# One-pass fillers of 512 columns for TensorE, at other places, and a later fourth weight piece

## The chip, the cores and the metric

The kernel runs on one core of a Trainium2 chip. The metric is the device time of one execution in microseconds (us); the median of three runs stands for it, 677.03 us before the change. A profile of one execution, with every instruction's start and duration, goes with it.

## What is computed

Two blocks in a row. The first is a gated linear recurrence over 768 steps, for 4 batches and 8 heads of 48 channels, with a complex gate for each step and channel; the second is a layer with one hidden activation, x·cos(x).

```python
mag = sqrt(a_re * a_re + a_im * a_im)
scale = minimum(mag, 0.999) / (mag + 1e-06)
a = (a_re + 1j * a_im) * scale             # per batch, head, step, channel
for t in range(S):                         # S = 768
    state = a[t][:, None] * state + outer(k[t], v[t])
    y[t] = q[t] @ real(state)
x = y, heads side by side                  # 3072 x 384
h = x @ w_in                               # 384 -> 2048
out = (h * cos(h)) @ w_out                 # 2048 -> 384
```

The inputs are float32, but the two weights arrive as 64-bit floats and are turned into 32-bit ones on the chip.

## The kernel before, in words

The steps are cut into chunks of 128 and two chunks make a group: 24 chunks, 12 groups. Within a chunk the recurrence is turned into matmuls: cumulative sums of the log gate and of its angle (products with a triangular matrix: `lgs` and `phs` in PSUM), keys and queries scaled by powers, cosines and sines of them (`ks`, `qs`), their transposes (`kT`, `qT`), the scores (`sc`), a masked copy of those (`atm`), the state that is carried on (`sp`, `state`), and the outputs. In group 0 these come as rows (`yr`, copied to `rows`) and are transposed (`xp`) to columns (`xT`); in later groups they are made as columns (`yp`). The second block is `mm1` (`hp`, eight pieces jp of 256 hidden columns, then cosine on ScalarE, a square sum `junk` on ScalarE, and a product on VectorE into `gate`) and `mm2` (`op`).

Nearly everything up to the first full group is a long prologue, and the change lies in it. What sets its order:

- `matmul` (L683) chains every TensorE instruction to the one before it, so TensorE runs in the order in which the program lists it. ScalarE's special functions are chained too. As long as `Ordered.by_hand` is true (L1225 to L1247), so is all of VectorE and ScalarE. After that a scheduler orders VectorE's and ScalarE's other work by where it is listed and by which operands it needs; each engine then takes its instructions strictly in that order.
- The weights are fetched in 16 pieces of 768 KB by GpSimd's DMA queue, eight of `w_in` (0 to 7 here) and eight of `w_out` (8 to 15), into four buffers (`raw`). A piece is converted in four steps (`as_floats`, L619): a shift and an or on VectorE (`TENSOR_SCALAR`, `SCALAR_TENSOR_TENSOR`), an addition of a constant on ScalarE (`raw<-raw`), and a final addition on VectorE (`CUSTOM_DVE_ANT_0`). That frees the buffer for the piece four places later. Pieces 0 to 3 are `early[0]` to `early[3]`, listed by hand in the loop at L1248; the others are woven in from L1257 on.
- `busy(count)` (L686) issues TensorE products whose result nobody reads. They take a PSUM buffer of the five that `pa` has. Here they are full float32 products of two constants, 128 columns wide; a float32 product shows in the trace as two MATMUL records and two weight loads. The trace lists TensorE's granted clock, 1.00 or 0.50 of full speed.
- The calls of `busy`: 12 ahead of everything (L1227), 8 after the sums of each of the two chunks (L1233), 12 after the trigonometric steps (L1243).

Of the kernel before, what the change touches and what calls it, by code (L numbers as in the profile page):

```python
# [11 lines left out]
F32 = mybir.dt.float32  # L12
# [3 lines left out]
F32R = mybir.dt.float32r  # L16
# [471 lines left out]
def fast_path(ctx, tc, q, k, v, a_re, a_im, moe_w_in, moe_w_out, out, least, odd, wide):  # L488
# [6 lines left out]
    nc = tc.nc  # L495
    B, H, S, D = q.shape
    DM, DF = moe_w_in.shape
    C = 128
# [21 lines left out]
    stage = {"pool": room.enter_context(tc.tile_pool(name="stage", bufs=1)), "bufs": 4}  # L520
    pa = ctx.enter_context(tc.tile_pool(name="pa", bufs=5, space=PSUM))
# [11 lines left out]
    def constant(array, name, queue=nc.scalar, pool=consts):  # L533
        t = pool.tile(list(array.shape), F32, name=name)
        queue.dma_start(out=t, in_=nc.inline_tensor(array, name=name + "_const").ap())
        return t
# [13 lines left out]
    def load(g, names, i=None, put=nc.sync.dma_start):  # L550
        for name in names:
            ap = {"re": a_re, "im": a_im, "q": q, "k": k, "v": v}[name]
            if name not in X[g]:
                X[g][name] = ld.tile([C, G, H, D], F32, tag=name, name=name,
                                     bufs=2 if name == "v" else 1)
            b, c = divmod(g * G + (i or 0), NCH)
            one, n = i or 0, G if i is None else 1
            steps = ap[b].rearrange("h (c p) d -> p c h d", p=C)[:, ds(c, n)]
            tile_ = X[g][name][:, ds(one, n)]
            parts = [(0, C, 0)]  # L560
            if name in ("re", "im") and g >= PEG:

                parts = [(0, C - 16, 1), (C - 16, C - 1, 1)]
                put(out=tile_[C - 1:C], in_=steps[0:1])
            for i_ in range(n):
                for lo, hi, by in parts:
                    put(out=tile_[lo:hi, i_], in_=steps[lo + by:hi + by, i_])

    for names in ("re", "im"), ("k", "q"), "v":
        for i in range(G):  # L570
            load(0, names, i)
    ident = constant(np.eye(C, dtype=np.float32), "ident", pool=stage["pool"])
    sums = [constant(sums_np[0], "sums", pool=stage["pool"])]
# [20 lines left out]
    def weight(dst, src):  # L594
        if src.dtype == F32:
            nc.sync.dma_start(out=dst, in_=src)
            return lambda: None
        return from_double(dst, src)
# [50 lines left out]
    def chain(ins, engine="scalar"):  # L649

        if engine in tail:
            behind(ins, tail[engine])
        tail[engine] = ins
# [29 lines left out]
    def matmul(out, **kw):  # L683
        chain(nc.tensor.matmul(out, **kw), "tensor")  # L684

    def busy(count):  # L686

        ps = pa.tile([C, C], F32, tag="a", name="busy")
        for _ in range(count):
            matmul(ps, lhsT=ident, rhs=sums[0], start=True, stop=True)  # L690

    tables = {AF.Ln: "natural_log_exp_and_others", AF.Exp: "natural_log_exp_and_others",
              AF.Arctan: "trig_and_small", AF.Sin: "trig_and_small"}
# [2 lines left out]
    def preload(table):  # L696
        if loaded[0] != table:
            loaded[0] = table
            chain(nc.scalar.preload_act_table_set(table))  # L699
# [87 lines left out]
    def p_powers(g, i):  # L787

        x = X[g]
        if i == 0:  # L790
            x["P"], x["Q"] = x["lg"], temp("Q")
            x["row"] = rows_d.tile([G * DM], F32, tag="row", name="row")
            x["end"] = ft.tile([D2, G * H], F32, tag="end", name="end")
        ps = pa.tile([C, DM], F32, tag="a", name="lgs")
        summed_up(ps, g, i, "lg", sums[0])
        special(out=cut(x["P"], i, 1), in_=ps, func=AF.Exp)
        special(out=cut(x["Q"], i, 1), in_=ps, func=AF.Exp, scale=-1.0)
# [22 lines left out]
    def p_end(g, i, n):  # L820
        end = X[g]["end"][:, ds(i * H, n * H)]
        vector.tensor_scalar(out=end, in0=end, scalar1=-0.5, scalar2=None, op0=ALU.mult)
        low = least[:, ds(i * H, n * H)]
        vector.scalar_tensor_tensor(out=low, in0=end, scalar=LEAST, in1=low,
                                    op0=ALU.is_ge, op1=ALU.min)
# [40 lines left out]
    def g_trig(g, i, n):  # L866
        x = X[g]
        if i == 0:
            x["cos"] = temp("rs")
            if g:  # L870
                x["sin"] = temp("lg")
        cs, sn = cut(x["cos"], i, n), cut(x["sin"], i, n)
        ph = cut(x["tan"], i, n)
        vector.tensor_scalar(out=cs.bitcast(U32), in0=ph.bitcast(U32),
                                scalar1=0x7FFFFFFF, scalar2=None, op0=ALU.bitwise_and)
        special(out=sn, in_=ph, func=AF.Sin, scale=TWO_PI)
        special(out=cs, in_=cs, func=AF.Sin, scale=-TWO_PI, bias=half_pi_b)
# [44 lines left out]
    def queries(n, h):  # L922
        g, i = divmod(n, G)
        if g < PEG:
            return X[g]["qT"][:, i * H + h].rearrange("p q j -> p (q j)")
        return X[g]["qT"][:, :, i * H + h]
# [32 lines left out]
    def f_rows(n):  # L959

        y, (g, i) = Y[n], divmod(n, G)
        state = y.get("state")
        ps = pa.tile([C, H, D], F32, tag="a", name="yr")
        for h in range(H):
            matmul(ps[:, h], lhsT=y["atm"][:, h], rhs=X[g]["v"][:, i, h],
                   start=True, stop=(state is None))
            if state is not None:
                matmul(ps[:, h], lhsT=queries(n, h), rhs=state[:, h], start=False, stop=True)
        y["rows"] = msb.tile([C, DM], F32, tag="ot", name="rows")
        scalar.copy(out=y["rows"], in_=ps.rearrange("p h d -> p (h d)"))  # L970

    def f_columns(n):
        y, (g, i) = Y[n], divmod(n, G)
        ps = pa.tile([C, ND, C], F32, tag="a", name="xp")
        for c in range(ND):
            chain(nc.tensor.transpose(ps[:, c], y["rows"][:, ts(c, C)], ident), "tensor")
        if i == 0:
            X[g]["xT"] = msb.tile([C, ND, G, C], F32, tag="xT", name="xT")
        scalar.copy(out=X[g]["xT"][:, :, i], in_=ps)

    def f_state(n):
        if n % NCH == NCH - 1:
            return
        y, (g, i) = Y[n], divmod(n, G)
        ps = pa.tile([D2, H, D], F32, tag="a", name="sp")
        for h in range(H):
            keys = X[g]["ks"][:, i * H + h].rearrange("p a d -> p (a d)")
            matmul(ps[:, h], lhsT=keys, rhs=X[g]["v"][:, i, h], start=True, stop=True)
        new = ft.tile([D2, H, D], F32, tag="state", name="state")
        end = X[g]["end"][:, ts(i, H)].unsqueeze(2).to_broadcast([D2, H, D])  # L990
        if "state" in y:
            vector.scalar_tensor_tensor(out=new, in0=ps, scalar=0.25, in1=y["state"],
                                           op0=ALU.mult, op1=ALU.add)
            vector.tensor_tensor(out=new, in0=new, in1=end, op=ALU.mult)
        else:
            vector.scalar_tensor_tensor(out=new, in0=ps, scalar=0.25, in1=end,
                                           op0=ALU.mult, op1=ALU.mult)
        Y[n + 1]["state"] = new
# [162 lines left out]
    def turned(g, i, name):  # L1161
        return [lambda hh=hh: f_turn(g, i, name, hh) for hh in range(2)]
# [60 lines left out]
    early = [weight(dst, src) for dst, src in into[:RAW]]  # L1223
    chain(nc.gpsimd.tensor_copy(out=exact, in_=ones), "gpsimd")
    Ordered.by_hand = True  # L1225
    preload("natural_log_exp_and_others")
    busy(12)  # L1227
    one, two = (log_steps(0, i, 1) for i in range(2))
    for _ in range(5):
        next(one), next(two)  # L1230
    for i in range(2):
        p_powers(0, i)
        busy(8)  # L1233
    next(one), next(two)
    g_angle(0, 0, 2)
    for i in range(2):
# [3 lines left out]
    g_trig(0, 0, 1)  # L1240
    p_apply(0, 0, 1)
    g_trig(0, 1, 1)
    busy(12)  # L1243
    g_stack(0, 0, 1)
    p_apply(0, 1, 1)
    g_stack(0, 1, 1)
    Ordered.by_hand, Ordered.mark = False, dict(tail)  # L1247
    for t in (turned(0, 0, "kT") + turned(0, 0, "qT") + early[:1]  # L1248
              + [lambda: f_scores(0, 0), lambda: f_scores(0, 1)] + early[1:2]
              + turned(0, 1, "kT") + turned(0, 1, "qT") + early[2:3]  # L1250
              + [lambda: p_end(0, 0, 2), lambda: f_state(0), lambda: f_rows(0)] + early[3:4]
              + [lambda: f_scores(1, 0), lambda: f_scores(1, 1), lambda: f_columns(0)]
              + [lambda: f_state(1), lambda: f_rows(1), lambda: f_columns(1)]
              + [lambda: next(one, None), lambda: next(two, None),
                             lambda: load(2, ("v",))]):
        t()
# [95 lines left out]
```

## Time and profile before

| | |
|---|---|
| median of 3 runs | 677.03 us (676.07, 677.03, 678.66) |
| profiled execution, first to last instruction | 677.3 us |
| TensorE busy | 647.8 us, 96% |
| VectorE busy | 490.3 us, 72% |
| ScalarE busy | 396.4 us, 59% |
| granted clock below full speed | 11.8 to 15.2, 42.5 to 52.7, 69.8 to 73.2 us, and at the very end |

The profiled execution has no time of its own beside its span; the span lies 0.3 us above the median. "Idle before" in a line of the trace is written in brackets, with what ended it: `[0.94 <-DVE atm L673]` means that the engine sat idle for 0.94 us until VectorE had written `atm`. DVE is VectorE, ACT ScalarE, PE TensorE, PEld its weight load, POOL GpSimd, SP SyncE. All VectorE operations that go through the ordering helper carry its line, L673, and all matmuls L684, so they are told apart by their tiles.

### The profile page before, as it was taken

Reading aid. Unit: us, or ns where it says so; the run is one execution under the profiler, and the core shown is the slowest. Engines: PE = TensorE matmul, PEld = TensorE weight load, DVE = VectorE, ACT = ScalarE, POOL = GpSimd, SP = SyncE. Lnnn points to the kernel's source line nnn. Section 1 sums busy time; section 2 is a strip of 40 time slices with the busy share of each in tenths; the row PEclk is TensorE's granted clock in tenths of the full one; section 3 lists DMA queues with packets and bytes.
Section 4 is the critical chain, followed back from the end, with each engine's and each line's share of the span. In section 5 each row is a group of like instructions: output and inputs, shape, how many; then the busy total and the mean of one; then the engine's idle time right before and its main releaser. Section 6 shows DMA issues by size and latency. Waiting matters only on the chain.

```text
span 677.3 us, 10771 instructions
## 1 busy us (share of the span) xinstructions
PE 647.8 (96%) x4080; PEld 580.3 (86%) x4080; DVE 490.3 (72%) x792; ACT 396.4 (59%) x730; POOL 28.5 (4%) x47
## 2 busy tenths in 40 slices
PE   5788889999999999999999999999999999999995
PEld 5686657886799999999999999989999989999895
DVE  4879888759868778868768778868768769762251
ACT  5869775475466467367467467467367467432330
POOL 2011100000000000000000000000000000000000
PEclk8979899999999999999999999999999999999998
DMA  9778623923743864764864864854864753363000
GB/s 244 176 234 224 173 72 81 227 66 69 213 92 63 219 137 116 210 142 109 224 140 118 210 140 113 214 113 126 223 145 118 211 138 78 116 139 116 24 6 24
DMA packets 232810, 94.90 MB, mean 140 GB/s; under 512 B 208798, under 2 KB 221217, under 8 KB 232748
## 3 DMA queue, kind: packets, MB, share of 16 engines
q1 hardware_dynamic: 226252, 68.62, 44.5%
q0 software_dynamic: 5632, 25.17, 11.4%
q8 instruction: 34, 0.56, 0.4%
q10 hardware_dynamic: 864, 0.33, 0.2%
q14 instruction: 28, 0.23, 0.1%
HBM read 69.28 MB, written 24.81 MB: 139 GB/s over the span
## 4 chain that ended last, share of the span: by engine, by line
PE 79%; DVE 6%; DMA 6%; ACT 5%; issue 2%; SPq 1%; DVEq 0%; ACTq 0%
PE hp L684 32%; PE sum L684 15%; PE op L684 14%; PE yp L684 5%; PE sc L684 5%; PE sp L684 3%; PE phs L684 2%; DVE w_in L673 1%; PE lgs L684 1%; DMA raw<-in_moe_w_out_dram 1%; DMA xT<-x 1%; DMA qT<-moved 1%; DVE mag L673 1%; PE yr L684 1%; ACT L699 1%
## 5 line engine op out<-in xcount | busy, mean ns | idle before, releaser
L684 PE MATMUL hp<-xT,w_in 128*128 128x256 f32 x1152 | 254.2, 382 | 1.3 <-ACT xT L673 0.6
L684 PEld LDWEIGHTS hp<-xT,w_in 128*128 128x128 f32 x1152 | 219.9, 192 | 34.6 <-DMA xT<-x 1.9
L703 ACT ACTIVATE gate<-hp,half_pi_b 128x512 f32<-128x512 f32 x96 | 65.9, 686 | 128.0 <-PE hp L684 128.0
L673 DVE TENSOR_TENSOR gate<-hp,gate 128x512 f32<-128x512 f32 x96 | 65.5, 683 | 58.4 <-ACT junk L673 58.4
L684 PE MATMUL op<-w_out,gate 128*128 128x192 f32 (+1 forms) x448 | 103.0, 375 | 2.7 <-DVE w_out L673 2.7
L684 PEld LDWEIGHTS op<-w_out,gate 128*128 128x128 f32 x448 | 75.7, 190 | 19.7 <-DVE w_out L673 3.9
L673 ACT ACTIVATE junk<-hp 128x512 bf16<-128x512 f32 x96 | 56.5, 588 | 0.0
L684 PE MATMUL sum<-t_s,s 128*128 128x192 f32 x320 | 55.3, 326 | 0.0
L684 PEld LDWEIGHTS sum<-t_s,s 128*128 128x128 f32 x320 | 52.6, 190 | 0.0
L673 DVE TENSOR_TENSOR atm<-sc,causal 128x512 f32<-128x512 f32 x48 | 33.0, 687 | 25.4 <-PE sc L684 25.2
L684 PEld LDWEIGHTS sc<-qT,kT 96*128 96x128 f32 x384 | 47.6, 192 | 4.2 <-issue 2.2
L684 PE MATMUL sc<-qT,kT 96*128 96x128 f32 x384 | 49.4, 276 | 1.9 <-ACT qT L673 0.9
L673 ACT ACTIVATE ot<-sum 128x192 f32<-128x192 f32 x30 | 9.5, 320 | 49.4 <-PE sum L684 49.4
L699 ACT ACT_TABLE_LOAD x26 | 33.4, 1283 | 4.0 <-DMA ident<-ident_const 3.6
L673 ACT CAST tan<-phs 128x384 int32<-128x384 f32 x24 | 11.5, 479 | 39.7 <-PE phs L684 39.7
L673 DVE SCALAR_TENSOR_TENSOR ot<-op,ot 128x192 f32<-128x192 f32 x31 | 11.0, 354 | 32.3 <-ACT ot L673 23.5
L684 PE MATMUL yp<-atm,v 128*48 128x128 f32 x352 | 33.5, 277 | 0.0
L684 PEld LDWEIGHTS sp<-v,ks 128*96 128x96 f32 x320 | 29.7, 165 | 0.0
L684 PE MATMUL sp<-v,ks 128*96 128x48 f32 x320 | 29.6, 245 | 0.0
L684 PE MATMUL sum<-w_out,gate 128*128 128x192 f32 x160 | 29.6, 329 | 0.0
L684 PE MATMUL yp<-qT,state 96*48 96x128 f32 x304 | 29.6, 272 | 0.0
L684 PE MATMUL op<-t_a,gate 128*128 128x192 f32 x160 | 29.0, 332 | 0.0
(137 smaller groups left out, 992.7 us busy)
## 6 DMA issues: line engine op xcount, KB each, us to landing
moved<-tr SPq DMA_DIRECT2D x20, 768.0 KB
raw<-in_moe_w_in_dram POOLq DMA_DIRECT2D x16, 768.0 KB, 5.5
raw<-in_moe_w_out_dram POOLq DMA_DIRECT2D x16, 768.0 KB, 4.9
kT<-moved SPq DMA_DIRECT2D x40, 192.0 KB
qT<-moved SPq DMA_DIRECT2D x10, 768.0 KB
k<-in_k_dram SPq DMA_DIRECT2D x24, 192.0 KB
q<-in_q_dram SPq DMA_DIRECT2D x24, 192.0 KB
v<-in_v_dram SPq DMA_DIRECT2D x24, 192.0 KB
```

Of the source, the lines that this page charges most:

```text
L673: ins = getattr(self.engine, op)(**kw)
L684: chain(nc.tensor.matmul(out, **kw), "tensor")
L699: chain(nc.scalar.preload_act_table_set(table))
L703: chain(nc.scalar.activation(func=func, **kw))
```

## The change

The fillers become products in the one-pass format (`float32r`) of a tile of ones, 512 columns wide, instead of float32 products of the constants `ident` and `sums`. The tile `idle` is new and is set by VectorE ahead of its other first writes. The counts and places change: 27 at the start instead of 12; none between the two chunks' sums, and 10 after both instead of 8 and 8; 10 instead of 12 after the trigonometric steps; and three new groups around the second chunk's rows, of 4, 2 and 2. The conversion of piece 3 (`early[3]`) is listed behind the rows of chunk 1 instead of ahead of its scores.

```diff
+    idle = stage["pool"].tile([C, 512], F32, name="idle")
+    nc.vector.memset(idle, 1.0)
     for names in ("re", "im"), ("k", "q"), "v":
...
     def busy(count):
 
-        ps = pa.tile([C, C], F32, tag="a", name="busy")
+        ps = pa.tile([C, 512], F32, tag="a", name="busy")
         for _ in range(count):
-            matmul(ps, lhsT=ident, rhs=sums[0], start=True, stop=True)
+            matmul(ps, lhsT=idle[:, 0:C].bitcast(F32R), rhs=idle.bitcast(F32R),
+                   start=True, stop=True)
...
-    busy(12)
+    busy(27)
     one, two = (log_steps(0, i, 1) for i in range(2))
     for _ in range(5):
         next(one), next(two)
     for i in range(2):
         p_powers(0, i)
-        busy(8)
+    busy(10)
     next(one), next(two)
...
     g_trig(0, 1, 1)
-    busy(12)
+    busy(10)
     g_stack(0, 0, 1)
...
-              + [lambda: p_end(0, 0, 2), lambda: f_state(0), lambda: f_rows(0)] + early[3:4]
+              + [lambda: p_end(0, 0, 2), lambda: f_state(0), lambda: f_rows(0)]
               + [lambda: f_scores(1, 0), lambda: f_scores(1, 1), lambda: f_columns(0)]
-              + [lambda: f_state(1), lambda: f_rows(1), lambda: f_columns(1)]
+              + [lambda: f_state(1), lambda: busy(4), lambda: f_rows(1)] + early[3:4]
+              + [lambda: busy(2), lambda: f_columns(1), lambda: busy(2)]
```

The built programs show what this does to the order. TensorE's order is the same but for the fillers. On VectorE the three conversion steps of piece 3 move from between `end` and the last `atm` of chunk 1 to after both `atm` and the first step of chunk 1's state. On ScalarE, piece 5's step moves behind the copy of `rows`, piece 6's step moves three places forward, and piece 9's step moves from ahead of the fourth `gate` to behind the fifth. Further small moves follow up to the start of group 2; from there on all engines' orders are as before.

## Prediction

> **What bounds it now.** I read the table by stages first. From 123 us on TensorE is busy for 51 of every 51 us at full clock, and from group 2 on the orders are unchanged; so the change is worth what it moves the start of that stretch (122.39 us, the third group's first `hp`). Ahead of it, the table at the clock's own windows:
>
> ```profile
> 8.34:11.76 3.42, 0.59 (x6) 0.40 (x4) 2.18 (x6) 3.36 (x8) 2.67 (x4) 0.96 1.09 241
> 11.76:15.17 3.41, 3.07 (x11) 2.46 (x12) 2.43 (x6) 2.83 (x7) 0.00 (x0) 0.54 1.05 331
> ...
> 39.07:42.48 3.41, 2.46 (x24) 2.37 (x23) 3.41 (x6) 2.26 (x4) 0.73 (x2) 0.96 1.12 341
> 42.48:45.90 3.42, 3.42 (x18) 3.42 (x17) 3.20 (x6) 2.64 (x3) 0.15 (x1) 0.50 1.00 369
> 45.90:49.30 3.40, 2.26 (x9) 1.61 (x9) 0.18 (x1) 2.47 (x5) 0.00 (x0) 0.50 0.69 162
> ```
>
> Busy time of PE, PEld, DVE, ACT, POOL, then clock. A window with little TensorE work is followed by half clock. In 45.90 to 49.30 VectorE, full until then, works 0.18 us. The timeline says why:
>
> ```profile
> 15.99 0.81 PE L684 MATMUL lgs<-lg,sums 128*128 128x384 f32 x2
> 16.83 0.49 ACT L703 ACTIVATE lg<-lgs 128x384 f32<-128x384 f32 x1 [2.18 <-PE lgs L684]
> ```
> ```profile
> 40.85 0.39 PE L684 MATMUL yr<-v,atm 128*128 128x48 f32 x2 [0.94 <-DVE atm L673]
> ```
> ```profile
> 46.67 0.48 ACT L673 COPY rows<-yr 128x384 f32<-128x384 f32 x1 [1.52 <-PE yr L684]
> ```
> ```profile
> 49.40 0.96 DVE L673 SCALAR_TENSOR_TENSOR mag<-re,mag 128x768 f32<-128x768 f32 x1 [3.31 <-ACT mag L703]
> ```
> ```profile
> 62.28 1.04 ACT L673 ACTIVATE raw<-raw,carrier_b 128x768 uint32<-128x768 uint32 x1 [1.49 <-DVE w_in L673]
> ```
>
> First, ScalarE waits 2.18 us for chunk 1's sums, which stand behind eight fillers. Second, the rows of chunk 1 start late behind `atm`, run at half clock, and hold ScalarE's queue, and VectorE's 3.31 us with it. Third, ScalarE waits 1.49 us for piece 9 (VectorE was done, so its fetch). The chain of waits runs through VectorE, ScalarE and the fetches until about 97 us, through TensorE's last `op` products (95.93, behind `w_out`), then to 122.39. VectorE idles only some 7 us between 24 and 98; that and an earlier start are all there is to gain.
>
> **The skill.** The Trainium skill, "TensorE: Matmul & The Clock Gate", Part 1: the clock is halved after an idle activity window of 3.4 us and restored after a busy one, in a free-running grid. The trace agrees: all its spells are multiples of 3.41 us on one grid. Its threshold I take from the trace. At full clock `hp` takes 20.72 us for 96 records of 256 columns, 0.216 us each, so 48 columns stream in 0.041 us a record, 0.081 a product, while `yr` products come every 0.222 us: 36% streaming. Window 39.07 to 42.48 held 0.36 us of that from `sp` and 0.59 from `yr`, 28%, and the clock fell; 18.58 to 22.00 held two sums of 0.64, 37%, and it stayed. Same page, "Back-to-back issue gap": N/2.4 + 2.5 ns, 216 ns for 512 columns. The one-pass sums before (384 columns) start 0.173 us apart, 0.23 for 512 scaled; I take 0.23, and 0.43 to 0.46 at half clock.
>
> **Part by part.** I lay the new order on each engine with the timeline's start-to-start distances: VectorE 0.87 us for 768 columns, 0.47 for a shift, 0.60 for `atm` and `gate`; ScalarE 0.90 for a piece, 0.74 to 0.93 for a 768-column function, 0.58 and 0.57 for `gate` and `junk`, 1.30 for a table.
>
> *Start.* `idle` costs VectorE one write of 512 columns. The trace has none; the 128x512 product at 0.68 us is the upper end, 0.1 the lower. TensorE's queue waits for it, so it begins at about 1.4 us instead of 4.12, since no constant is awaited; nothing else of it is due before 12.1. If full clock comes at a grid point between 4.9 and 8.3, 27 fillers end between 9.4 and 11.0 us, ahead of 12.1: free. Never coming, they would end at 13 to 14. *No fillers between the sums.* The second sum's input is ready at 13.52, its product then ends at 14.5 (15.1 at half clock) instead of 16.80. ScalarE: two exponentials to 15.5 to 16.1, table load 1.30, arctangent from 17.4 at the latest (before 19.02). It does not gain all: VectorE is next late, with its six power steps from 16.74 to 19.88, which do not move. The ten fillers end by 17.3, free. First phase subtraction 19.80 instead of 21.38, second 21.88 instead of 23.45: −1.57 us. The ten after it (2.3 us) end at 23.7, before the transposes at 25.0: free.
>
> *To 38 us* VectorE and TensorE are dense and shift by 1.57; keys and queries landed by 10.9 us and the four first pieces by 21.4, so no transfer holds this back. Piece 2's conversion ends at 36.48.
>
> *Piece 3 listed later.* Gone from ahead of chunk 1's `atm`: 0.47 + 0.87 + 0.87 us (start to start). `end`, then `atm` 36.7 to 37.4 (its scores are there), `state` to 37.9, second `atm` to 38.5. TensorE's `sp` ends at 38.3; four fillers 38.15 to 39.1, on the path: 0.8 us (their PSUM buffer is the one that chunk 0's rows left, copied out by 35.4, so they wait for nothing more). So `yr` starts at 39.1 (before 40.85). At full clock 16 products at 0.222 and the drain, 3.7 us, instead of 5.80: ends 42.75 (46.65), −3.9. The two groups of two fillers (0.46 each) lie beside ScalarE's copies of 0.48: free. The moved steps run on VectorE from 38.9 to 43.1, with 0.5 us of waiting for group 1's angle input. GpSimd's fetch of piece 7 queues behind them, at 43.1 instead of 41.87; it is needed at 57: free. SP's queue gets nothing new.
>
> *ScalarE then:* rows 42.75, piece 5 43.1, `xT` 44.05, log 44.45, piece 6 45.3, `mag` 46.2 (48.52), second log 47.7 (50.89; piece 6 no longer stands before it), exponential to 50.9 (54.10), table, first `gate` 52.2 (55.42). VectorE idles 44.9 to 47.1 instead of 3.31 us, then runs: gates at 53.6, 55.6, 59.2, 60.7; the fourth −3.8, with as much converted. `hp` starts 4.1 us earlier, but that alone is worth nothing, since its fourth piece waits for the first gate's PSUM.
>
> *Piece 9 behind the fifth gate.* The 1.49 us goes: fourth gate on ScalarE 57.45 (63.20), group 1's exponentials 59.95 (65.75), arctangent 62.9 (68.70), phases 63.8 (69.60), which I price at half clock again, 2.9 us, after 3.0 us of idling; at full clock 1.3. VectorE keeps less of that, since its conversions stand in between and only 3 us of idling are left to remove: eighth gate 80.3 (86.04), then pieces 12 to 15, each 2.21. Piece 15 can be fetched once piece 11 is done: 83.05 + 0.56 + 4.6 (before's last fetch: 88.14 to 92.69) = 88.2, and is wanted at 88.3, hardly a wait. Done at 92.3 (96.7); group 2's first step, now ahead of its last conversion step, at 90.5 (96.66). TensorE finishes `op` at 93.0 instead of 98.6: −5.6. VectorE's line is at −6.1; TensorE's is the later one, so 122.39 becomes 116.8.
>
> Sum: −1.57 at the start, −2.3 at the rows and the queue behind them, −1.7 at piece 9 and the order around it: −5.6. Against the profiled 677.3 us that is 671.7; the median is 0.3 lower: 671.4, say **671.5**.
>
> **Rivals.** (a) The clock falls in `yr` all the same: a window that lies almost wholly in it holds 36 to 38%, and nothing shows the threshold between 28 and 37. At worst 12 of 16 products at 0.43: `yr` ends near 45.3, ScalarE 2.5 us later: −3.1, 673.8. For it: 3.7 us of `yr` are longer than a window. Against: six of the eight new fillers stand at its edges. (b) The start's gain goes as well: a half-clock spell between 12 and 19 us makes the fillers end after the arctangent (10 x 0.46 from 15 us is 19.6, which takes it all): −1.5, 675.5. (c) Slower: products of ones in one pass do not count as activity; nothing in the trace shows that they do. Then 27 fillers end at 13 to 14 (+1.5), the ten after the sums at 20 to 21, the phases take 1.65 instead of 0.93 and the last ten 4.6, so that the transposes start at about 29 instead of 26.56, and they and the scores at half clock add 2 before they warm it themselves; the later list gives 1.85 back: +3, 680. It decides once the delay before 35 us exceeds some 2 us. (d) The phases at 63.8 come at full clock: −1.6 there, of which half may last: 670.
>
> **Numbers.** Forecast 671.5: 0.56. (a) 0.22, (b) 0.10, (c) 0.05, (d) 0.07. 0.5% is 3.4 us, about what a measurement tells from no change: faster is below 673.65, nearly all of the forecast, (d) and a third of (a), 0.69; slower (c), 0.05; the same 0.26. The unknown write and filler rates move it 0.3 us, the clock's phase 1 to 1.5. The range 669.8 to 675.2 leaves out (c), half of (b) and the tails.
>
> **What would show it.** Clock 1.00 through 39 to 46 us; `yr` starting at about 39 and ending before 43; ScalarE's wait for `lgs` gone and first phase near 18; VectorE's wait for `mag` near 2 us; no wait for piece 9; `hp` of the third group near 116.8. It is wrong if the fillers' clock stays 0.50, or if `op` still waits for a fetch near 95.

## The result, and the profile after

| | before | after |
|---|---|---|
| median (runs) | 677.33 us (4: 676.07 to 678.66) | 674.88 us (4: 673.82 to 675.38) |
| profiled execution: span | 677.3 us | 673.0 us |
| profiled execution: its own time | not recorded | 674.87 us |
| half clock before 100 us | 11.8 to 15.2, 42.5 to 52.7, 69.8 to 73.2 | 13.2 to 16.6, 43.9 to 47.3, 64.4 to 67.8, 84.9 to 88.3 |

A fourth run of the kernel before is in its median here. The recorded ratio is 0.9947, with a 95% interval of 0.9922 to 0.9973: about half a per cent faster. It is an estimate over the runs and not the quotient of the medians, which is 0.9964: the ratio stands for 3.6 us of 677.3 and its interval for 1.8 to 5.3, and the two medians of four differ by 2.45. The forecast was 671.5 us with a range of 669.8 to 675.2; the time lies inside, 3.4 us above the forecast and 0.3 us below the end of the range.

The table at the clock's own windows, of the profile after (stretch, its length, busy us of PE, PEld, DVE, ACT and POOL with counts, clock, DMA share, GB/s):

```profile
2.94:6.35 3.41, 3.41 (x10) 2.69 (x9) 0.52 (x1) 2.22 (x3) 0.00 (x0) 1.00 1.27 252
6.35:9.76 3.41, 3.41 (x17) 2.70 (x15) 1.34 (x4) 2.86 (x6) 2.34 (x5) 1.00 1.33 215
...
13.17:16.59 3.42, 3.10 (x7) 2.16 (x8) 3.28 (x7) 2.77 (x7) 0.00 (x0) 0.54 1.03 363
...
37.06:40.48 3.42, 3.36 (x28) 2.84 (x28) 3.42 (x8) 2.30 (x4) 0.42 (x1) 1.00 1.14 327
40.48:43.89 3.41, 3.37 (x27) 2.94 (x27) 2.86 (x6) 2.73 (x4) 0.41 (x1) 0.96 0.65 246
43.89:47.30 3.41, 3.41 (x11) 2.59 (x10) 0.84 (x1) 3.39 (x6) 0.35 (x1) 0.53 1.05 274
```

The trace has no record of the clock ahead of 6.35 us, and the table prints 1.00 there; the number of fillers in a window, 10 and then 17, shows that the clock was half until then. The products of ones alone bring full clock, so they count as activity. `yr` (39.2 to 43.0) now runs at full clock, and the fall comes right after it. The timeline of TensorE from the start:

```profile
1.46 8.60 PE L686 MATMUL busy<-idle 128*128 128x512 f32 x27 [1.46 <-DVE one_b L540]
12.02 0.91 PE L686 MATMUL lgs<-lg,sums 128*128 128x384 f32 x2 [1.96 <-DVE lg L675]
13.49 1.65 PE L686 MATMUL lgs<-lg,sums 128*128 128x384 f32 x2 [0.56 <-DVE lg L675]
14.37 3.68 PE L686 MATMUL busy<-idle 128*128 128x512 f32 x10
18.26 1.56 PE L686 MATMUL phs<-tan,turns 128*128 128x384 f32 x4 [0.21 <-ACT tan L706]
```

and the first phase products in the profile before:

```profile
19.91 1.56 PE L684 MATMUL phs<-tan,turns 128*128 128x384 f32 x4 [1.33 <-ACT tan L703]
```

The second sum follows its input at 13.49 instead of standing behind fillers until 15.99, and the first phase products start at 18.26 (before: 19.91). The ten fillers end at 18.05, 0.21 us ahead of the work: free, but only just. Around the rows of chunk 1, TensorE first, then ScalarE and VectorE:

```profile
37.98 1.18 PE L686 MATMUL busy<-idle 128*128 128x512 f32 x4
39.22 0.42 PE L686 MATMUL yr<-v,atm 128*128 128x48 f32 x2
...
42.60 0.39 PE L686 MATMUL yr<-state,qT 96*128 96x48 f32 x2
```
```profile
43.03 0.48 ACT L675 COPY rows<-yr 128x384 f32<-128x384 f32 x1 [0.66 <-PE yr L686]
```
```profile
47.42 0.96 DVE L675 SCALAR_TENSOR_TENSOR mag<-re,mag 128x768 f32<-128x768 f32 x1 [2.68 <-ACT mag L706]
```

The copy of `rows` starts 3.64 us earlier, and VectorE's wait for `mag` falls from 3.31 to 2.68 us. Further on TensorE's phases of group 1, the late `op` products, and the third group:

```profile
64.38 1.65 PE L686 MATMUL phs<-tan,turns 128*128 128x384 f32 x2 [2.88 <-ACT tan L706]
```
```profile
84.00 2.36 PE L686 MATMUL op<-w_out,gate 128*128 128x384 f32 x4 [3.14 <-DVE w_out L675]
86.16 1.06 PE L921 MATMUL tp<-ident,ks 128*96 128x128 f32 x4
...
92.27 2.75 PE L686 MATMUL op<-w_out,gate 128*128 128x384 f32 x8
94.86 0.60 PE L921 MATMUL tp<-ident,qs 128*96 128x128 f32 x4
```
```profile
117.76 4.58 PE L686 MATMUL hp<-xT,w_in 128*128 128x256 f32 x20
```

The last two of these places in the profile before:

```profile
98.61 0.60 PE L918 MATMUL tp<-ident,qs 128*96 128x128 f32 x4
...
122.39 2.86 PE L684 MATMUL hp<-xT,w_in 128*128 128x256 f32 x12
```

The last `op` products end at 94.86 (before: 98.61), where the transposes `tp` behind them start, and the third group starts 4.63 us earlier (122.39). From there to the end it is 555.2 us (554.9). So the profiled executions differ by 4.3 us and the medians by 2.45.

### The profile page after: what moved, and what is told of

Read it like the earlier page. It is cut to its first block, busy times and chain, and to the rows that moved or that the text cites. A ratio compares the mean times of both kernels' runs of the same rounds, so it can differ in the third digit from the quotient of the medians.

```text
span 673.0 us, 10725 instructions
## 1 busy us (share of the span) xinstructions
PE 649.9 (97%) x4055; PEld 579.6 (86%) x4055; DVE 490.5 (73%) x793; ACT 396.5 (59%) x730; POOL 27.8 (4%) x47
## 4 chain that ended last, share of the span: by engine, by line
PE 80%; ACT 6%; DVE 6%; DMA 6%; issue 2%; SPq 0%; ACTq 0%; DVEq 0%
PE hp L686 32%; PE op L686 17%; PE sum L686 14%; PE yp L686 6%; PE sc L686 5%; PE sp L686 3%; PE phs L686 2%; DMA re<-in_a_re_dram 1%; PE lgs L686 1%; ACT raw L675 1%; DMA qT<-moved 1%; DMA raw<-in_moe_w_in_dram 1%; DVE mag L675 1%; DMA raw<-in_moe_w_out_dram 1%; DVE tan L675 1%
## 5 line engine op out<-in xcount | busy, mean ns | idle before, releaser
L686 PEld LDWEIGHTS op<-w_out,gate 128*128 128x128 f32 x448 | 75.9, 191 | 19.7 <-DVE w_out L675 4.1
L686 PEld LDWEIGHTS sum<-t_s,s 128*128 128x128 f32 x320 | 52.5, 191 | 0.3 <-DVE ot L675 0.3
L675 ACT CAST tan<-phs 128x384 int32<-128x384 f32 x24 | 11.5, 478 | 39.2 <-PE phs L686 39.2
```

The costliest lines, as they stand in the source:

```text
L675: ins = getattr(self.engine, op)(**kw)
```

## The experiments

**Theory.** The gain comes by the steps of the forecast: chunk 1's sums and `yr` start earlier, and the end of the prologue is set by VectorE's conversions, not by the clock. What is missing from 5.6 us is partly that the profiled execution of before was slower than its median. **Rival.** The gain is the clock's: the fillers keep TensorE at full speed, the moves in place are worth little, and filling the gaps that are left would bring the rest.

Each run is compared with runs of the kernel before on the same chip; there were three groups, with a median of before of 677.97, 677.54 and 678.80 us. In the table, the four kernels after the first line belong to the first group, the next four to the second, the last two to the third. The ratios are the recorded estimates, as above; "below before" in the text is a difference of means within a group. "Half clock" is 2 x (1 - mean clock) x span, the time that a run spent at half clock; it includes a stretch at the very end, after TensorE's work, and leaves out the start, for which the traces have no record of the clock. The slope is that of a straight line through all runs of a kernel, time over half clock; its standard error is 0.04 to 0.13, and 0.23 where both gaps are filled without the late fillers.

| kernel | median (runs) | ratio, 95% interval | mean half clock | slope |
|---|---|---|---|---|
| before (41, 48 and 43 runs) | 677.97, 677.54, 678.80 | | 19.6 to 19.7 us | 0.30, 0.32, 0.44 |
| before, unchanged | 677.86 (14) | 1.0004, 0.9987 to 1.0021 | 19.7 | 0.32 |
| piece 3 later, alone | 675.90 (22) | 0.998, 0.9969 to 0.9992 | 18.9 | 0.27 |
| all new fillers, piece 3 in its old place | 674.75 (9) | 0.9962, 0.9945 to 0.9979 | 12.3 | 0.24 |
| changed, without the late 4, 2 and 2 | 673.72 (9) | 0.9951, 0.9933 to 0.9969 | 17.6 | -0.04 |
| early fillers new, alone | 677.17 (22) | 0.9999, 0.9981 to 1.0017 | 21.7 | 0.37 |
| old fillers, place alone | 677.18 (22) | 0.9995, 0.9981 to 1.001 | 20.1 | 0.41 |
| changed, unchanged | 674.38 (8) | 0.9952, 0.9932 to 0.9971 | 11.3 | 0.06 |
| without the late ones, both gaps filled | 673.69 (9) | 0.9943, 0.9921 to 0.9964 | 13.7 | 0.02 |
| changed, both gaps filled | 676.91 (22) | 0.9969, 0.9956 to 0.9983 | 7.3 | 0.09 |
| changed, second gap filled | 675.84 (22) | 0.9961, 0.995 to 0.9972 | 10.8 | 0.13 |

### How the measurement itself moves

The kernel before once more, with no edit.

> The kernel before, unchanged, for its own spread. Theory one: the profiled execution of before (span 677.3) was an unlucky one, because the clock's grid of 3.41 us is free-running and its phase decides where half clock falls in chunk 1's rows; device times exceed spans by about 1.9 us as in the runs after, so typical spans of before lie near 675.4, between 674 and 677, and this profile shows half-clock spells at other places than 42.5 to 52.7. Rival: before's spans are near 677.3 each time and the extra 1.9 us arise with the change only; then the spans here come out at 677.0 to 677.6.

677.86 us (14 runs), ratio 1.0004; runs of before on one chip differ by up to 6.4 us (674.95 to 681.35 in the third group). Spans go from 673.6 to 679.7 us in these 14 runs, so the rival, 677.3 each time, falls. In its profile the half-clock stretches lie at 11.5 to 18.3, 45.6 to 52.5 and 69.5 to 72.9 us: one window more at the start than in the first profile of before, and one less at the rows. Its third group starts at 121.61 us, against 122.39. So a single profile of this kernel is one draw, and differences below about a microsecond need many runs.

The changed kernel once more:

> The changed kernel, unchanged, for more runs of it beside those of before. Theory (spans of before vary by 3 us with the phase of the clock's grid, and its profile was 1.1 us above the middle one): time 674.5 to 675.2, 3 us or 0.45% under before, and a smaller spread than before's 1.3. Rival (the first four runs were slow by chance and the profiles' difference of 4.3 is the true one): 673.5.

674.38 us (8 runs), ratio 0.9952, as at first. Its profile has half clock at 14.3 to 17.7 and 65.5 to 68.9 only, none behind `yr` and none at 85 us; its third group starts at 117.44 us, against 117.76. Two stretches of half clock less came with 0.3 us. Its runs spread with a standard deviation of 0.52 us; those of before in the same group with 1.27.

### One part at a time

Piece 3 later, nothing else:

```diff
-              + [lambda: p_end(0, 0, 2), lambda: f_state(0), lambda: f_rows(0)] + early[3:4]
+              + [lambda: p_end(0, 0, 2), lambda: f_state(0), lambda: f_rows(0)]
...
-              + [lambda: f_state(1), lambda: f_rows(1), lambda: f_columns(1)]
+              + [lambda: f_state(1), lambda: f_rows(1)] + early[3:4] + [lambda: f_columns(1)]
```

> Only the later listing of piece 3; all fillers as before. Theory one (the parts act in a chain, ScalarE and VectorE pass on what each frees): rows of chunk 1 start about 1.0 us earlier (TensorE's sp ends 39.9 instead of the wait to 40.85), half clock stays, piece 9 leaves the place before the fourth gate; third group's hp 1.5 to 2.5 us earlier, time 675 to 676. Rival (the clock is everything): no change within 0.5 us, 677.

675.90 us, ratio 0.998 (0.9969 to 0.9992); by the means 1.6 us below before, with hardly less half clock (18.9 us), as the theory had it. Not as expected, the fall of the clock comes behind `yr` here too, with no filler to help it; TensorE's timeline of this run:

```profile
40.28 0.39 PE L684 MATMUL yr<-v,atm 128*128 128x48 f32 x2
...
43.63 0.39 PE L684 MATMUL yr<-state,qT 96*128 96x48 f32 x2
44.87 0.90 PE L976 MATMUL xp<-ident,rows 128*128 128x128 f32 x3 [0.85 <-ACT rows L673]
```

All records of `yr` take 0.39 us (in the profile before: 0.39, then 0.63 from 42.59 on). It starts right behind `sp` without the 0.94 us for `atm`.

All new fillers, piece 3 in its old place (the diff of the change without its two lines on `early[3:4]`):

> All of the new fillers, piece 3 at its old place. Theory one: start 1.6 us earlier, yr starts at 39.3 to 39.6 and keeps full clock to its end at 43.2, but piece 9 stands before the fourth gate again and its wait is back; third group's hp about 2.5 to 3 us earlier than before, time 675.5. Rival (the clock is everything): all of the gain, 674.9 or less.

674.75 us, ratio 0.9962: the number falls on the rival's side, all of the gain. Its `yr` starts at 39.65 and its third group at 118.17 us. ScalarE's wait ahead of the fourth `gate` is back, but with 0.64 us (before: 1.49). With its standard error of 0.40 it can't be told from the changed kernel. That the clock is not everything is shown by the next run.

The changed kernel without the late fillers:

```diff
-              + [lambda: f_state(1), lambda: busy(4), lambda: f_rows(1)] + early[3:4]
-              + [lambda: busy(2), lambda: f_columns(1), lambda: busy(2)]
+              + [lambda: f_state(1), lambda: f_rows(1)] + early[3:4]
+              + [lambda: f_columns(1)]
```

> The changed kernel without the three new groups of 4, 2 and 2 fillers. Theory one: yr starts at 38.2 instead of 39.2, and the clock falls in it or after it at the next grid point, which costs 0 to 2 us of yr by the grid's phase; on average the same as the changed kernel within 0.7 us, with a larger spread: 674.2 to 675.6. Rival (the late fillers hold the clock and that is the gain): 1.5 us more than the changed kernel, 676.4.

673.72 us, ratio 0.9951. `yr` starts at 38.21 instead of 39.22 us: the four fillers cost 1.0 us on the path, as the forecast had it (0.8). In exchange they take 6.3 us of half clock away (17.6 to 11.3), and that buys nothing here: against its own before the kernel without them is 3.7 us down in the mean, the changed kernel 3.15, a difference of 0.6 with a standard error of 0.45. This is the strongest point against the rival: at the slope of before, 0.34 over all 132 runs, the changed kernel's 8.4 us less half clock would come to 2.9 us, nearly its whole gain, but this kernel gains as much with 2.0 us less. What does change is the spread, 0.95 to 0.52 us.

Only the early fillers (27, none between, 10 and 10, in one pass), no late ones, piece 3 as before:

```diff
-    busy(12)
+    busy(27)
...
-        busy(8)
+    busy(10)
...
-    busy(12)
+    busy(10)
```

> Only the start's new fillers (27, none between the sums, 10, 10, one-pass); no late fillers, piece 3 at its old place. Theory: the start's 1.6 us are kept to the third group nearly whole, since nothing else moves: 676.2, about 1.6 under before. Rival (the late fillers of the fillers-only kernel gave a good half of its 3.0 us, by full clock through chunk 1's rows): then this stays at 676 or above; if it comes out at 675 or under, the late fillers gave nothing there either.

677.17 us, ratio 0.9999, the runs from 672.99 to 682.59: no gain on average, where 676.2 was expected, and a wider spread (standard deviation 2.39) that follows half clock. Its profile had 13.1 to 20.0 at half clock, two windows, and TensorE's timeline shows what that does:

```profile
13.62 1.65 PE L686 MATMUL lgs<-lg,sums 128*128 128x384 f32 x2 [0.52 <-DVE lg L675]
14.49 5.04 PE L686 MATMUL busy<-idle 128*128 128x512 f32 x10
19.33 1.65 PE L686 MATMUL phs<-tan,turns 128*128 128x384 f32 x4
```

The ten fillers take 5.04 us instead of 3.68, and the phases have no idle time before them: they wait for the fillers, not for the arctangent, until 19.33 us. That is rival (b) of the forecast, in part: 1.07 of the 1.65 us gained are lost in this run.

The old fillers, all sixteen behind both sums:

```diff
     for i in range(2):
         p_powers(0, i)
-        busy(8)
+    busy(16)
```

> The kernel before with its two groups of 8 fillers put behind both sums as one group of 16; float32 products of 128 columns as before. Theory: the second sum's wait behind fillers is what the start gains from, so the same 1.6 us: 676.2. Rival (the one-pass products matter at the start): no gain within 0.5 us, 677.6.

677.18 us, ratio 0.9995, the runs from 674.22 to 680.9. That is the rival's number; but the one-pass fillers at the same places, above, gain nothing either, so the rival's reason is not borne out. The correlation of time with mean clock is -0.91: the five runs with 14.8 us at half clock took 674.2 to 675.1 us, the three with 25.8 us or more 679.9 to 680.9. In its profile, a good draw, the second sum's exponential comes at 15.3 us and the third group at 119.3, 3.1 us earlier than in before's first profile; on average next to nothing of that is left.

One more run of each of these kernels, to see whether the lines through their earlier runs hold:

> The start's new fillers only, one more look at another phase of the grid. Theory (time before the third group follows the time at half clock, 0.37 us for 1 us of it over 22 runs of this kernel): time within 2 us of 669.4 + 0.37 x T, T the time at half clock in this execution; where T is over 22, the half-clock spells lie over the start's sums and phases (12 to 20 us) and over chunk 1's rows. Rival: no such relation, time anywhere in 673 to 682.

676.08 us at a clock of 0.986 and a span of 674.3: 18.9 us at half clock, and the line gives 676.4.

> The place change only (16 old fillers behind both sums), one more look at another phase. Theory: time within 1.5 us of 668.8 + 0.41 x T, from 22 runs of this kernel; where T is over 22, the fillers behind the sums run at half clock past the arctangent's end and the first phase sum waits for them, 20 us or later. Rival: no such relation.

675.29 us at 0.988 and 673.5: 16.2 us, and the line gives 675.4. Both lie within 0.4 us of the line. Two points fit the dependence; neither had more than 22 us at half clock, so they don't show where in the program the bad draws lose their time.

### Filling the gaps that are left

If the half clock at 64 and 85 us cost time, fillers in the idle time ahead of it should gain. Eight go ahead of group 1's first phase products, ten ahead of the second of four `op` groups, in the changed kernel without its late fillers:

```diff
-          (phases(1), 0.7, 0.8), (keys(1), 0.8, 0.9), (convert(back[:4]), 0.5, 1.0))
+          ([lambda: busy(8)], 0.7, 0.72), (phases(1), 0.72, 0.8), (keys(1), 0.8, 0.9), (convert(back[:4]), 0.5, 1.0))
...
+          ([lambda: busy(10)], 0.235, 0.245),
```

> The changed kernel without the three late groups, and with fillers in the two gaps after which the clock fell in its profile instead: 8 ahead of group 1's first phase sum (gap 61.5 to 64.4) and 10 ahead of the second four products of op, which wait for piece 11 (gap 80.9 to 84.0). Theory: op, the transposes and the last scores keep full clock and TensorE reaches the third group's hp 0.5 to 1.5 us sooner than without: 672.8. Rival (VectorE's conversions set that end alone): the same as without the late fillers, 673.7 to 674.1.

673.69 us (9 runs), ratio 0.9943, where 672.8 was expected. Its profile has no half clock between 47.4 us and the very end and its third group at 116.46, the earliest seen (117.47 without the gap fillers); but by the runs it can't be told from the kernel without them (0.9951), nor from the changed one (0.9952).

The same two groups added to the changed kernel itself:

> The changed kernel with its late fillers, and with the fillers in both gaps (8 ahead of group 1's first phase sum, 10 ahead of the products of op that wait for piece 11). Theory (op and transposes at half clock cost the changed kernel 1 us in most phases): 673.3, spread under 0.8, half clock 8 us or less. Rival (VectorE's conversions alone set that end): 674.4 as the changed kernel.

676.91 us (22 runs), ratio 0.9969: slower than theory and rival had it, 2.1 us below before where the changed kernel was 3.15. The profiled run was at full clock from 17.5 to 672.9 us, and yet its third group starts at 117.98, not earlier than 117.76. TensorE's timeline there:

```profile
64.55 0.91 PE L686 MATMUL phs<-tan,turns 128*128 128x384 f32 x2 [1.06 <-ACT tan L706]
```
```profile
91.42 1.46 PE L686 MATMUL op<-w_out,gate 128*128 128x384 f32 x4
93.68 1.56 PE L686 MATMUL op<-w_out,gate 128*128 128x384 f32 x4 [0.80 <-DVE w_out L675]
95.07 0.60 PE L921 MATMUL tp<-ident,qs 128*96 128x128 f32 x4
```

The phases run at full clock (0.91 us instead of 1.65). At the end of the prologue TensorE now waits 0.80 us for VectorE's last conversion, which in the profile after had not been waited for, since half clock had used up that time. In all seven profiles of kernels with piece 3 moved the last `op` products end 1.45 to 1.48 us after VectorE's last conversion does, whether the clock was half at 85 us (three of them) or not (four). So a full clock between 64 and 95 us is worth nothing in these profiles: VectorE sets the end. The rival falls for this stretch.

Only the second gap filled:

> The changed kernel with the 10 fillers ahead of op's waiting products alone. Theory: this gap is the one on the path, so the same 673.3 to 673.6 as with both. Rival (the phase sums' gap is the one that counts): 674.2 or more.

675.84 us (22 runs), ratio 0.9961; its third group starts at 117.68. No gain either, against an expected 673.3 to 673.6. By the means it is 0.96 us (standard error 0.30) faster than the kernel with both gaps filled. Why the eight fillers at 61 us cost that is not settled: they run while TensorE has nothing else (61.32 to 63.5, the phases wait another 1.06 us), and the same eight did no such harm without the late ones. Part of what the profile of the kernel with both gaps lost is in its later part: from the third group's start to the end it has 558.3 us, the changed kernel 555.2. VectorE and TensorE in one group there:

```profile
508.31 0.56 DVE L675 TENSOR_SCALAR raw<-raw 128x768 uint32<-128x768 uint32 x1 [1.93 <-DMA raw<-in_moe_w_out_dram]
```
```profile
512.72 0.44 PE L686 MATMUL lgs<-lo,exact 128*128 128x384 f32 x1 [0.76 <-DVE lo L675]
```

and VectorE in the same place of the profile after, where it does not wait:

```profile
504.89 0.59 DVE L675 TENSOR_SCALAR raw<-raw 128x768 uint32<-128x768 uint32 x1
```

The weights are fetched a second time in this later part, piece by piece, to look at their exponents (`guard`, L631 in the kernel after). One such fetch, issued at 501.91, landed at 508.31, 6.4 us later (after: 4.5 to 4.7 us in the same stretch). VectorE, in order, held back the log steps behind it, and TensorE's `lgs` with them. From 125 us on VectorE waits 9.9 us in all for such fetches in this profile, and 6.1 to 6.9 us in those of before, of after and of its repeat. Whether the kernel with both gaps has more of it as a rule one profile can't say. No version tried beats the changed kernel by more than its interval.

## Why the prediction was right, and where its size was off

The range held on its upper side by 0.3 us. That side was laid out for rivals (a) and half of (b), and neither came in the changed kernel, so part of this is luck: the forecast change was 5.5 us and the measured one is 2.45 by the medians, 3.6 by the ratio. The forecast also gave 0.69 to a time below 673.65, and it is 674.88. The steps, in the profile:

| step | forecast | measured | forecast less measured |
|---|---|---|---|
| 27 fillers end | 9.4 to 11.0 | 10.1 | |
| first and second phase subtraction | 19.80, 21.88 | 19.73, 21.80 | 0.1 |
| `yr` starts; rows copied | 39.1; 42.75 | 39.22; 43.03 | -0.1; -0.3 |
| VectorE's wait for `mag` | 2.2 | 2.68 | -0.5 |
| fetch of piece 7 | 43.1 | 43.48 | -0.4 |
| first gate, ScalarE | 52.2 | 52.69 | -0.5 |
| fourth gate, ScalarE | 57.45 | 57.94 | -0.5 |
| phases of group 1 | 63.8 | 64.38 | -0.6 |
| eighth gate, VectorE | 80.3 | 81.06 | -0.8 |
| last conversion ends, VectorE | 92.3 | 93.4 | -1.1 |
| last `op` ends | 93.0 | 94.86 | -1.9 |
| third group's `hp` | 116.8 | 117.76 | -1.0 |

**The start: right in the profile, not by itself.** The -1.57 us came as -1.65, with the wait of 2.18 us for `lgs` down to 0.61. The fillers start 0.427 us apart at half clock and 0.227 us apart at full clock, where the forecast took 0.43 to 0.46 and 0.23; the formula that it quotes gives 0.216, and the measured figure is the one to use. As a gain of its own the step failed: the early fillers alone are 0.1 us below before (standard error 0.5) and the place alone 0.5 (0.5), where 1.57 was forecast. With piece 3 later it is worth 2.1 us (standard error 0.4: 676.24 to 674.10 in means of one group). The forecast added the three steps as if each held alone.

**The rows: right.** The clock held through `yr`, with the forecast's copy of the rows 0.3 us early. The four fillers cost 1.0 us on the path against 0.8. That they are needed was not right: piece 3's move alone, and the kernel without the late fillers, kept `yr` at full clock in their profiles. Late fillers and piece 3's move are substitutes: where piece 3 stays, the late fillers are worth 2.8 us (0.1 against 2.9 us below the means of before, standard error 0.7); where it moves, they are worth nothing (0.6 us slower, standard error 0.45).

**ScalarE's queue and piece 9: right, with 0.2 us more on the way.** The wait for piece 9 is gone and the phases of group 1 came at half clock, 2.88 us after TensorE's last work, as priced. To the 0.3 us of the rows 0.2 us are added up to the first gate, with the transposes `xp` at half clock (0.86 us). Rival (d), phases at full clock, came in the kernel with both gaps filled, and its third group is not earlier. (The forecast's 670 for (d) does not follow from its terms: half of 1.6 us below 671.5 is 670.7.)

**The end of the prologue: the term that was mis-sized.** The forecast wrote "TensorE finishes `op` at 93.0 instead of 98.6: −5.6." This is 0.7 us after its own last conversion (92.3), but the last four `op` products need that conversion and take 1.4 us. The repeat of the changed kernel shows it where the clock is full:

```profile
93.14 1.56 PE L686 MATMUL op<-w_out,gate 128*128 128x384 f32 x4 [0.76 <-DVE w_out L675]
94.54 0.60 PE L921 MATMUL tp<-ident,qs 128*96 128x128 f32 x4
```

Its last conversion there is this, so that it ends at 93.09:

```profile
92.13 0.96 DVE L675 CUSTOM_DVE_ANT_0 w_out<-raw,w_out 128x1536 uint16<-128x1536 uint16 x1
```

The other 1.1 us are VectorE's. In the profile after:

```profile
71.41 0.69 DVE L675 TENSOR_TENSOR gate<-hp,gate 128x512 f32<-128x512 f32 x1 [0.64 <-ACT junk L675]
...
92.43 0.95 DVE L675 CUSTOM_DVE_ANT_0 w_out<-raw,w_out 128x1536 uint16<-128x1536 uint16 x1
```

0.5 us are there from the first gate on, and at 71.41 it waits 0.64 us for ScalarE. From there to 93.38 it is busy for 21.63 of 21.97 us, so nothing can be caught up. Half clock at 84.9 to 88.3 us, which looks like the cause in the profile after, is not: without it `op` ends at 94.54 to 95.07. Of the 1.9 us, 0.9 came back that the forecast had not priced: from the end of `op` to the third group it took 23.78 us before and takes 22.90 now. Some 0.6 us of this lie at the sums `lgs`, whose wait for `lo` (0.35 us at 105.83 before) is gone; the log step of group 2 that leads to them now stands ahead of the last conversion step. The other 0.3 lie right ahead of the third group's first `hp`. The forecast has no wait there, but in six profiles, all of kernels that lack the new early fillers, the later piece 3 or both, this product waits 0.19 to 0.91 us for the transfer that fills `xT`, and in none of the six profiles of kernels with both parts. The shift is -4.6 instead of -5.6.

**The base: the larger miss.** "The profiled execution has no time of its own" led to taking the span, 677.3 us, for the time. In all runs where both are recorded the time is 1.73 to 1.98 us above the span. So the profiled execution of before should have taken about 679.1 us (an estimate; none of the four recorded runs is as long), 1.8 us over the median of 677.33. A shift of 4.3 us from there gives 674.8, and the median after is 674.88. Of the 3.4 us between forecast and result, 1.8 are this base, 0.3 the step from the span to the median that went the wrong way, 1.0 the shift and 0.3 the later part (554.9 to 555.2 us).

**What made that execution slow** is known in part only. Time follows half clock in before with 0.30 to 0.44 us for each us, but that execution had 20.7 us of it, 1.0 more than the mean of before, which makes 0.3 to 0.4 of the 1.8 us. The rest is open. The Trainium skill, "TensorE: Matmul & The Clock Gate", Part 1, says that the activity window is free-running and that the ramp penalty is below 1% of a typical span. The first agrees with the two profiles of the changed kernel, whose first stretch of half clock starts at 13.2 and at 14.3 us. So does the second: runs of before had 14.8 to 28.4 us of half clock, which makes 4.6 us at a slope of 0.34, 0.7%. But the change measured here is half a per cent, so the penalty can't be left out of account. The slope is 0.24 to 0.44 in the kernels with neither or only one of the two parts, new early fillers and piece 3 later, and -0.04 to 0.13 in all kernels with both. With their standard errors this sets the kernels with both apart from before and from the early fillers alone; the 0.24 of the kernel with all new fillers and piece 3 in its old place can't be told from them. That time hardly follows the clock where both parts are in is what the slopes show; through which wait is argued from the profiles, not shown.

**Rivals.** (a), the clock falling within `yr`, did not come. (b) came in part in the kernel with the early fillers alone. (c) fell with full clock at 6.35 us.

## What to carry to other kernels

Take the profiled execution's own time, not its span, and ask where it lies among the runs before adding a shift to a median; where TensorE's clock falls at places that differ from run to run, one profile is one draw. Edits that each remove a wait or a clock fall on the same path need not add: try each alone and each with the others. A stretch of half clock cost nothing here where VectorE was the last to arrive; look at who waits for whom at the end of the stretch before filling the idle time ahead of it.

## What the runs showed of the hardware

- One-pass products of a tile of ones, 512 columns wide, brought TensorE to full clock: at 6.35 us in one profile of the changed kernel and at 7.46 in the other, after a start at 1.46 in both. 27 of them took 8.60 and 9.10 us.
- The share of time in which columns stream does not seem to decide alone whether the clock holds. In 40.48 to 43.89 us of the profile after, ten `yr` products streamed for 0.81 us (at 0.081 us each, as in the forecast) and two fillers for 0.43 to 0.45 (0.216 to 0.227 us each): 36 to 37%, more with the transposes, and the clock fell; the forecast found 37% in a window that held. This is an estimate, and takes the windows to lie where the table has them. What the measure is stays open.
- The part after the prologue, the same instructions in each kernel from group 2 on, took 553.7 to 556.0 us in 13 profiles and 558.3 in one. That is as large a spread as the shift to be measured.
